# Splitting the last token tile's product and its evacuation into two column halves

## The chip, the cores and the metric

The kernel runs on one core of one Trainium2 chip. The metric is the device time of one execution in microseconds (us). I call the measured device time the clock. The profile shows one execution, whose span is some 1.7 us shorter than its device time. TensorE is PE in the profile, its weight loads PEld, VectorE is DVE, ScalarE ACT, GpSimd POOL, and SPq the queue from which the stores are issued.

All runs of more than one execution quoted here are of state fast; single runs have no state and are read from their traces alone. The sets of rounds ran on different chips, so a kernel is compared only with the kernel before of the same rounds.

## The reference, cut to what matters

A transformer block with modulation: sliding-window attention, then an MLP that mixes over tokens. Only the end of the MLP matters here (condensed from two functions).

```python
u = jnp.einsum('bsd,sf->bdf', h, w1) + b1      # S=2048 tokens, D=512, F=1792
u = _gelu(u)
y = jnp.einsum('bdf,fs->bds', u, w2) + b2      # second product: contracts F
x = x + gb * y.transpose(0, 2, 1)              # gate and residual, then out
```

## The kernel before

The output has 16 token tiles of 128 tokens by 512 columns. For each, TensorE sums 14 matmuls (128 rows of F each, 512 columns) into one PSUM buffer (pu). VectorE then does two instructions: f1, out of PSUM, adds b2 and multiplies by the gate; f2 adds the residual x and writes bf16 into an output buffer. A store of 128 KB sends it. The buffers o1 and otile rotate over three slots each.

```python
box["g"] = ctx.enter_context(tc.tile_pool(name="gtmp", bufs=3))
...
def e_f1(e, tb=tb):
    box["o1", tb] = box["g"].tile([P, D], F32, name="o1")
    ve.scalar_tensor_tensor(
        out=box["o1", tb][:], in0=ftiles[100 + tb], scalar=b2FM[:, tb : tb + 1], in1=bc_gb[:],
        op0=ALU.add, op1=ALU.mult,
    )

def e_f2(e, tb=tb):
    box["ot", tb] = box["g"].tile([P, D], BF, name="otile")
    ve.tensor_tensor(out=box["ot", tb][:], in0=box["o1", tb][:], in1=xres[tb][:], op=ALU.add)

def e_f3(e, tb=tb):
    sp.dma_start(out=out_dram[tb * P : (tb + 1) * P, :], in_=box["ot", tb][:])
```

The order of all pieces of work is a fixed list of numbers in the kernel; each engine works through its own instructions in that order. Its last entries read as follows (1366 is the residual add of tile 13, 1376 that of tile 14, 1378 to 1384 the last tile's matmuls in pairs, 1385 and 1386 its f1 and f2, 1367, 1377 and 1387 the stores of tiles 13, 14 and 15):

```
... 1373 1365 1357 1374 1380 1375 1381 1382 1376 1383 1366 1384
1385 1367 1377 1386 1387
```

So VectorE does tile 13's f1 (1365), tile 14's f1 (1375), and only then the two adds, 14's first.

The softmax here doesn't subtract the row's maximum and nothing guards it: scores larger than these inputs give would overflow.

## Time and profile before

| | before |
|---|---|
| device time, median | 267.24 us (267.21 to 267.50, 3 runs) |
| span of the profiled run (its device time 266.56) | 264.84 us |
| TensorE busy / VectorE busy | 94% / 73% |
| end of TensorE's last matmul | 260.60 us |
| last store issued / landed | 262.14 / 263.82 us |
| landing to the end of the span | 1.02 us |

The busy share of TensorE suggests that the body is bound by matmuls. The change is about the last 4.24 us, from the end of TensorE's last matmul to the end of the span; I call this stretch **R**. It is the sum of the wait and work on VectorE up to the last store's issue (1.54), the store's landing (1.68) and the closing waits (1.02).

### The profile page before, as it was taken

The page shows a single profiled execution, that of the slowest core. Times are in us where ns is not written, and L with a number is a line of the kernel's source. Part 1 is how long each engine was busy: PE and PEld are TensorE (multiplying, and loading weights), DVE is VectorE, ACT ScalarE, POOL GpSimd, SP SyncE. Part 2 cuts the span into 40 slices and gives each one's busy share as a digit, 9 for nine tenths or more (in the row PEclk, how much of TensorE's full clock was granted, in tenths as well). Part 3 has the DMA queues.
Part 4 walks back from the last instruction along what each step waited for, and adds up shares of the span by engine and source line. Part 5 has one row for each costly group of instructions (what it writes and reads, how often), then busy time and mean ns, then how long its engine had stood idle before and what let it go on. Part 6 is the DMA issues. An engine that isn't in the chain of part 4 may idle for free.

```text
span 264.8 us, 10695 instructions
## 1 busy us (share of the span) xinstructions
PE 248.2 (94%) x4769; PEld 136.8 (52%) x4769; DVE 193.5 (73%) x435; ACT 185.4 (70%) x268; POOL 95.9 (36%) x182
## 2 busy tenths in 40 slices
PE   7898999999998988899999999999999999999993
PEld 2576667656556654455544454445444444444441
DVE  5778896777847359999948888999998730415875
ACT  3479999999999899999999999999416431000000
POOL 8755321495289945553893031440000000000000
PEclk9999999999999999999999999999999999999999
DMA  7995400000017000000014862020499800001122
GB/s 212 369 382 197 42 5 6 2 5 2 2 49 196 5 4 5 2 2 2 5 38 128 227 172 85 2 61 23 152 362 397 360 2 0 21 0 63 59 99 79
DMA packets 31599, 25.35 MB, mean 96 GB/s; under 512 B 6076, under 2 KB 29632, under 8 KB 31552
## 3 DMA queue, kind: packets, MB, share of 16 engines
q1 hardware_dynamic: 31544, 24.66, 29.5%
q8 instruction: 37, 0.61, 0.9%
q14 instruction: 10, 0.08, 0.1%
q10 hardware_dynamic: 8, 0.00, 0.0%
HBM read 22.55 MB, written 2.10 MB: 93 GB/s over the span
## 4 chain that ended last, share of the span: by engine, by line
PE 67%; ACT 19%; DVE 8%; issue 4%; POOL 0%; ACTq 0%; POOLq 0%
PE pu L194 32%; ACT et L194 15%; PE pxy L194 13%; PE psa L194 8%; PE pq L194 5%; PE pa L194 4%; PE pv L194 3%; ACT lz L194 3%; DVE st L194 2%; DVE VT L194 1%; PE pt L194 1%; DVE part L194 1%; DVE OT L194 1%; PE psb L194 1%; DVE h L194 1%
## 5 line engine op out<-in xcount | busy, mean ns | idle before, releaser
L194 ACT ACTIVATE et<-psa 128x1536 bf16<-128x1536 f32 x75 | 109.1, 1455 | 4.0 <-PE psa L194 2.1
L194 PE MATMUL pu<-hb,w1p 128*128 128x512 bf16 x224 | 53.1, 380 | 0.8 <-DVE part L194 0.8
L194 PE MATMUL pu<-guT,w 128*128 128x512 bf16 x224 | 49.0, 379 | 0.0
L194 ACT ACTIVATE et<-psb 128x512 bf16<-128x512 f32 x75 | 45.1, 601 | 0.0
L194 PE MATMUL pxy<-et,ones_bd 128*32 128x192 bf16 (+3 forms) x960 | 38.7, 233 | 0.9 <-issue 0.9
L194 PE MATMUL pxy<-et,VT 128*32 128x192 bf16 (+3 forms) x960 | 38.4, 234 | 0.9 <-DVE OT L194 0.5
L194 PEld LDWEIGHTS <-w 128*128 128x128 bf16 x224 | 21.9, 98 | 26.4
L194 PE MATMUL psa<-QT,KT 32*128 32x192 bf16 (+3 forms) x720 | 29.8, 230 | 5.6 <-ACT et L194 4.9
L194 PEld LDWEIGHTS <-w1p 128*128 128x128 bf16 x224 | 20.3, 98 | 25.5 <-issue 2.3
L194 POOL TENSOR_SCALAR KT<-kb,mask_par 128x512 bf16<-128x512 bf16 (+1 forms) x36 | 22.9, 645 | 25.9 <-DVE kb L194 22.2
L194 PE MATMUL pq<-h1T,wqkv 128*128 128x512 bf16 (+1 forms) x128 | 30.1, 355 | 0.3 <-ACT VT L194 0.3
L194 PEld LDWEIGHTS <-KT 32*128 32x128 bf16 x960 | 16.1, 92 | 26.2 <-issue 23.9
L194 PEld LDWEIGHTS <-VT 128*32 128x32 bf16 x960 | 23.6, 96 | 11.6 <-issue 10.1
L194 PE MATMUL psb<-QT,KT 32*128 32x192 bf16 (+3 forms) x240 | 29.3, 231 | 0.0
L194 DVE SCALAR_TENSOR_TENSOR o<-pu,b2FM,bc_all 128x512 f32<-128x512 f32 x16 | 11.6, 748 | 20.2 <-PE pu L194 20.0
L194 DVE TENSOR_TENSOR et<-et,maskt 128x512 bf16<-128x512 bf16 (+2 forms) x56 | 24.9, 480 | 0.6 <-ACT et L194 0.5
L194 PEld LDWEIGHTS <-ones_bd 128*32 128x32 bf16 x960 | 23.2, 97 | 1.2 <-issue 1.1
L194 DVE BATCH_NORM_STATS2 st<-x 128x6 f32<-128x512 bf16 x32 | 21.7, 680 | 1.3 <-DMA x<-in_A_x_dram 1.1
L194 DVE TENSOR_TENSOR OT<-pxy,lz 128x256 bf16<-128x256 f32 x32 | 13.4, 420 | 10.6 <-ACT lz L194 10.1
L194 PEld LDWEIGHTS <-wqkv 128*128 128x128 bf16 x192 | 14.0, 97 | 13.4 <-issue 4.8
L194 PE MATMUL pv<-wqkv,h1T 128*32 128x256 bf16 x512 | 17.9, 274 | 0.2 <-DVE VT L194 0.2
L194 PE MATMUL pa<-wod,OT 128*128 128x512 bf16 x64 | 17.3, 381 | 0.3 <-ACT part L194 0.3
(113 smaller groups left out, 358.2 us busy)
## 6 DMA issues: line engine op xcount, KB each, us to landing
w1p<-in_B_w_dram SPq DMA_DIRECT2D x14, 512.0 KB, 6.1
w<-in_B_w_dram SPq DMA_DIRECT2D x14, 512.0 KB, 8.4
wmod<-in_w_mod_dram SPq DMA_DIRECT2D x6, 512.0 KB, 5.5
x<-in_A_x_dram SPq DMA_DIRECT2D x16, 128.0 KB, 4.8
out_dram<-otile SPq DMA_DIRECT2D x16, 128.0 KB, 1.7
wqkv<-in_A_wqkv_dram SPq DMA_DIRECT2D x2, 384.0 KB, 5.4
wqkv<-in_A_wqkv_dram SPq DMA_DIRECT2D x1, 512.0 KB, 5.0
wod<-in_A_wo_dram SPq DMA_DIRECT2D x1, 512.0 KB, 8.4
```

The costliest lines, as they stand in the source:

```text
L194: ins = call(*args, **kwargs)
```

## The change

The intent: the last tile's product is done in two column halves, each in a PSUM buffer of its own, the first half complete before the second begins. The first half's f1, f2 and store should go beside the second half's matmuls, so that only half of the evacuation follows TensorE's end. Its core (cuts marked):

```diff
-1385 1367 1377 1386 1387
+1367 1377 1385 1386 1387
...
+    def last_mm(e, n):
...
+        for m in range(4 * n, 4 * n + 4):
+            h, fc = divmod(m, NF)
+            te.matmul(
+                ftiles["last", h], lhsT=w2t[fc][:, (NT - 1) * P : NT * P], rhs=guT[fc][:, half * h : half * (h + 1)],
+                start=fc == 0, stop=fc == NF - 1, skip_group_check=True,
+            )
+
+    def last_out(h):
+        tb = NT - 1
+        cols = slice(half * h, half * (h + 1))
+        o1 = box["g"].tile([P, half], F32, name="o1h", tag="o1")
+        ot = box["g"].tile([P, half], BF, name="oth", tag="otile")
+        ve.scalar_tensor_tensor(
+            out=o1[:], in0=ftiles["last", h], scalar=b2FM[:, tb : tb + 1], in1=bc_gb[:, cols], op0=ALU.add, op1=ALU.mult,
+        )
+        ve.tensor_tensor(out=ot[:], in0=o1[:], in1=xres[tb][:, cols], op=ALU.add)
+        sp.dma_start(out=out_dram[tb * P : (tb + 1) * P, cols], in_=ot[:])
```

Both halves take their buffers from the same three slots as the whole tiles (tags o1 and otile). Entry 1385 of the list now stands for the first half's f1, f2 and store, 1386 for the second half's; so the halves' stores come after those of tiles 13 and 14.

More of the change, by code (lines that the diff above doesn't have):

```diff
@@ L1201 @@
         release(tag, ms, ge_ops[fc])
+    half = D // 2
+    def last_mm(e, n):
+        if n == 0:
+            for h in range(2):
+                ftiles["last", h] = box["ps_t"].tile([P, half], F32, name="pu1", tag=f"t{h}")[:]
+        for m in range(4 * n, 4 * n + 4):
[14 more added lines that the diff above has]
+        sp.dma_start(out=out_dram[tb * P : (tb + 1) * P, cols], in_=ot[:])
     fin_ops = {}
     for tb in range(NT):
+        if tb == NT - 1:
+            ms = []
+            for n in range(NF // 2):
+                ms.append(op("m2m", {"PE": 0.427}, lambda e, n=n: last_mm(e, n),
+                             deps=list(gu_ops.values()) + list(w2_ops.values()) + [fin_ops[t][0] for t in (10, 11)] + ms[-1:], pos=end + 17.0 + 3.0 * tb, cls="D"))
+            pos = end + 20.0 + 3.0 * tb
+            war = [fin_ops[t][2] for t in (tb - 3, tb - 2, tb - 1)]
+            f1 = op("f1", {"DVE": 0.76}, lambda e: last_out(0), deps=[ms[3]] + war, pos=pos)
+            f2 = op("f2", {"DVE": 0.76}, lambda e: last_out(1), deps=[f1, ms[-1]], pos=pos)
+            f3 = op("f3", {"SP": 0.64}, lambda e: None, deps=[f2], pos=pos, nbytes=64 * 1024)
+            fin_ops[tb] = (f1, f2, f3)
+            continue
         tag, ms = product("m2m", 100 + tb, [[(lambda fc=fc, tb=tb: w2t[fc][:, tb * P : (tb + 1) * P], lambda fc=fc: guT[fc][:]) for fc in (lo, lo + 1)]
```

## The prediction

> **What bounds the kernel now.** I first read the page's totals and its 40 slices (6.62 us each), to see which engine carries the last stage, then the chain of work that ended last, then the end of the timeline.
>
> ```profile
> PE 248.2 (94%) x4769; PEld 136.8 (52%) x4769; DVE 193.5 (73%) x435; ACT 185.4 (70%) x268; POOL 95.9 (36%) x182
> ...
> PE   7898999999998988899999999999999999999993
> ...
> DVE  5778896777847359999948888999998730415875
> ```
>
> The reader is to see two things. TensorE (PE) is busy nearly everywhere, so the body of the kernel is bound by it, and the change leaves its number of multiply-adds alone. In the last two slices VectorE (DVE) is at 7 and 5 tenths: at the very end it is not an idle engine waiting for the last product. The change can only act in the last microseconds, so the chain there is what counts:
>
> ```profile
> 5 pieces in order of time: start us, us, what
> 256.93 3.68 PE pu L194 x17
> 260.61 0.02 issue
> 260.63 0.76 DVE o L194
> 261.40 0.02 issue
> 261.42 0.69 DVE otile L194
> ```
>
> After TensorE's last matmul ends (260.61) come one scalar-tensor-tensor out of PSUM (o, bias and gate), one tensor-tensor (otile, the residual), then the store. This view ends at the last counted instruction; the store and the closing waits fill the rest of the 264.84 us. It suggests that TensorE's end releases everything, and that halving the two DVE instructions after it would save half of them. The timeline of VectorE over the same stretch shows why that is not so:
>
> ```profile
> 258.48 0.75 DVE L194 SCALAR_TENSOR_TENSOR o<-pu,b2FM,bc_all 128x512 f32<-128x512 f32 x1 [0.32 <-PE pu L194]
> 259.26 1.30 DVE L194 TENSOR_TENSOR otile<-o,x 128x512 bf16<-128x512 f32 x2
> 260.63 0.75 DVE L194 SCALAR_TENSOR_TENSOR o<-pu,b2FM,bc_all 128x512 f32<-128x512 f32 x1
> 261.42 0.69 DVE L194 TENSOR_TENSOR otile<-o,x 128x512 bf16<-128x512 f32 x1
> ```
>
> VectorE starts on token tile 14 at 258.48, then does the residual adds of tiles 14 and 13 until 260.56, and only then tile 15. Its work on the older tiles ends 0.05 us before TensorE's last matmul does: two chains end side by side. VectorE's backlog is as long as the product.
>
> The stores matter too. The timeline of the transfer queue over 260.5 to 260.9, and over 262.0 to the end:
>
> ```profile
> 260.58 0.33 SPq L194 DMA_DIRECT2D out_dram<-otile  x1
> ...
> 262.14 0.33 SPq L194 DMA_DIRECT2D out_dram<-otile  x1
> ```
>
> and the page's list of transfers (last column: us from issue to landing):
>
> ```profile
> out_dram<-otile SPq DMA_DIRECT2D x16, 128.0 KB, 1.7
> ```
>
> The first is the store of tile 13, whose landing the trace's records put at 262.30; one of tile 14 follows at 260.97 (lands 262.76); the last is that of tile 15, from 262.14 to its landing at 263.82. The span ends 1.02 us later.
>
> [...] the trace has 686 on average for otile. [...] the trace has a tensor-tensor of 256 columns:
>
> ```profile
> L194 DVE TENSOR_TENSOR OT<-pxy,lz 128x256 bf16<-128x256 f32 x32 | 13.4, 420 | 10.6 <-ACT lz L194 10.1
> ```
>
> [...] The trace has 216 between the starts of pu matmuls, and for four pq matmuls with 128x128 weights and 256 columns 0.60 us from first start to last end: (0.60 - 0.27)/3 = 0.11 between starts. So the doubled weight loads do not set the pace:
>
> ```profile
> 13.13 0.60 PE L194 MATMUL pq<-h1p,wqkv 128*128 128x256 bf16 x4
> ```
>
> [...] at the 160 GB/s or more that earlier slices show, 128 KB would move in under 0.8 us. I therefore expect a half-size store to land only slightly sooner. [...] Here VectorE is saturated for just these 2 us.
>
> **The change part by part.**
>
> TensorE: 14 matmuls of 512 columns become 28 of 256. 28 x 0.1085 = 3.04 against 14 x 0.216 = 3.02 us, so +0.02. The instruction listing shows 8 of the 28 before tile 14's last matmul, as 4 of the 14 were; so tile 14's release of VectorE stays within 0.01, and all ends near 260.63. The first half is complete 14 x 0.1085 = 1.5 us before that, about 259.1.
>
> VectorE: a scalar-tensor-tensor of 748 ns and a tensor-tensor of 686 become two of each with 256 columns. [...] 0.48 and 0.42. That is 1.80 for 1.43 us, +0.37.
>
> Buffers: the two halves take a slot each of the three otile slots, where the whole tile took one. The listing of waits shows that the first half's add waits for the store of tile 12 (landed 259.19, free), and the second half's add for the next store in order, tile 13's. That wait is new. Tile 13's store can't be issued before its add ends at 260.57, and this is unchanged.
>
> Now the times. The first half need not wait for the product, so it starts as soon as VectorE has issued tile 13's add: two adds in a row start 1.30 - 0.69 = 0.61 apart, so 259.87 + 0.61 = 260.48. Its add follows after 0.48 + 0.04 (a dependent pair starts 261.42 - 260.63 = 0.79 apart for a 0.75 first instruction): 261.00. The second half's first instruction starts 0.61 - 0.27 = 0.34 later, 261.34, long after its product is ready (260.63). Its add could go at 261.86. But tile 13's store lands at 262.30, and from a landing to the add that waits for it the trace has 0.09 (243.53 to 243.62). So it starts at 262.39, ends at 262.82 and its store is issued at 262.84: 0.70 later than the last store of before. I give the half-size store 1.62 instead of 1.68 to land. The sum is +0.70 - 0.06 = **+0.64 us**, and the clock for the whole program moves by the same.
>
> **The rivals.** (1) The intent works: the end follows the product, with 0.48 + 0.04 + 0.42 after it in place of 0.76 + 0.02 + 0.70. That would give -0.54, 266.7 us. Against it is the VectorE backlog: at 260.63 VectorE would be in the first half, which it started at 260.48 at the earliest. (2) VectorE alone is the bound and the buffer wait is harmless (another slot, or a store that lands sooner): the add goes at 261.86 and ends at 262.29, 0.17 later than the 262.12 of before; less 0.06 for the store, +0.1, 267.35 us. For it: the listing names only a transfer's lane, and I inferred the tile from the order of issue. (3) The 256-column matmuls are held up by their weight loads (98 ns busy each) and TensorE ends later: 28 x 10 ns would be 0.28, but 0.7 us of it are hidden behind VectorE, and only the 8 in front of tile 14's end push the rest, 0.08. (4) Two half stores (rows of 512 B in place of 1024 B) land no sooner or collide with the full stores of tiles 13 and 14: up to +0.1 to +0.3 more.
>
> **Range and chances.** 267.24 + 0.64 = 267.88; I say 267.85. The runs of before spread over 0.3 us, rival 2 lies at 267.35 and rival 4 at some 268.2, so 267.3 to 268.4 should hold 8 in 10. 2% is 5.3 us, more than everything from tile 14's first DVE instruction to the last landing except noise: same 0.98, each side 0.01.
>
> **What would show it.** Right: TensorE's last matmul ends at about 260.6 as before; VectorE shows four instructions of 128x256 of 0.48 and 0.42 us, the first starting near 260.5 without waiting for TensorE; the last add stands after an idle gap of some 0.5 us put down to a transfer out of otile; the last store is issued near 262.8. Wrong: the last add follows its partner at once (rival 2), or the span ends below 264.5, which would mean that VectorE had room for the first half before tile 13's add.

The forecast's sum came to +0.70 - 0.06 = +0.64 us. For 0.48 and 0.42, and for the 0.27 that follows from them, the trace of before gives the same values: an add takes 0.686 us at 512 columns and 0.420 at 256 (another tile's), 0.266 less, and 0.748 - 0.266 = 0.482 is then the estimate for f1. The 0.1085 us between the starts of matmuls of 256 columns lies within the 0.108 to 0.110 that the same trace has within its groups of pq matmuls. That a half-size store lands only slightly sooner was not shown: all 16 output stores of before have 128 KB, and the 1.62, so the -0.06 of the sum, is the author's guess. So are the 10 ns per matmul of rival 3 and the +0.1 to +0.3 of rival 4. "Saturated" stands for VectorE's 2.05 busy us of the 2.09 from 258.47 to 260.56.

## The result, and the profile after

The changed kernel took 267.88 us median (267.47 to 268.48, 4 runs); the kernel before, with one more run in the same rounds, 267.37 (267.21 to 267.59, 4 runs). The ratio is 1.002, with a 95% interval of 0.9998 to 1.0042. A ratio is the mean time of one kernel's fast runs over that of the other's of the same rounds, so not quite the ratio of the medians quoted. Kernels are compared only within the same rounds. By the 2% rule this is "same". The clock alone barely tells it from zero, so the traces decide.

First the totals and slices of the page of the changed kernel:

```profile
PE 249.0 (94%) x4783; PEld 138.2 (52%) x4783; DVE 194.2 (73%) x437; ACT 185.4 (70%) x268; POOL 95.8 (36%) x182
...
PE   7898999999989988799999999999999999999992
...
DVE  5768896777847559999948788999998730425865
```

There are 14 more matmuls and weight loads and 2 more VectorE instructions; nothing else in the body has changed. In the last slice VectorE still has 5 tenths, TensorE 2.

The end of the timeline of the changed kernel (start, duration, engine, instruction, count, and in brackets idle time before it and its releaser):

```profile
256.76 4.29 PE L194 MATMUL pu<-guT,w 128*128 128x256 bf16 x30
...
258.90 0.75 DVE L194 SCALAR_TENSOR_TENSOR o<-pu,b2FM,bc_all 128x512 f32<-128x512 f32 x1 [0.33 <-PE pu L194]
259.69 1.29 DVE L194 TENSOR_TENSOR otile<-o,x 128x512 bf16<-128x512 f32 x2
260.90 0.48 DVE L194 SCALAR_TENSOR_TENSOR o1h<-pu,b2FM,bc_all 128x256 f32<-128x256 f32 x1
261.41 0.42 DVE L194 TENSOR_TENSOR oth<-o1h,x 128x256 bf16<-128x256 f32 x1
261.75 0.48 DVE L194 SCALAR_TENSOR_TENSOR o1h<-pu,b2FM,bc_all 128x256 f32<-128x256 f32 x1
261.91 1.69 SPq L194 DMA_DIRECT2D out_dram<-oth  x2
262.82 0.42 DVE L194 TENSOR_TENSOR oth<-o1h,x 128x256 bf16<-128x256 f32 x1 [0.58 <-DMA out_dram<-otile]
```

TensorE ends at 256.76 + 4.29 = 261.05 (a merged row's duration runs from its first start to its last end). The first half starts at 260.90 without any wait on TensorE: its product was complete at 259.52 by the trace's records, but VectorE was at the adds of tiles 14 and 13 until then. So only 0.15 us of the first half's work lies beside the product. The second half's first instruction starts 0.71 after TensorE's end. Then VectorE stands idle for 0.58 us before the very last add, and what ends that idle time is a store out of otile.

The chain that ended last names the same thing:

```profile
260.30 0.70 DVE otile L194
261.00 0.02 issue
261.01 1.71 DMA out_dram<-otile
...
262.82 0.42 DVE oth L194
```

Before, the chain's last link to TensorE was the last matmul. Now it leads past it: tile 13's add (260.30), tile 13's store (1.71 us from issue to landing), the last add. None of TensorE's matmuls after 258.88, where tile 14's product ends, is on it. The view of the output's transfers matches only 12 of the 17 stores to their landings, and the last one is not among them. By the trace's records it is issued at 263.27 and lands at 264.80, 1.53 us later; the first half's store, which went while tile 14's was under way, took 1.62. R is 265.76 - 261.05 = 4.71 us, against 4.24 before. In parts: 2.22 up to the last issue (before 1.54), 1.53 of landing (1.68), 0.96 of closing waits (1.02); +0.68 - 0.15 - 0.06 = +0.47. TensorE's own time comes on top (next paragraph).

In this execution TensorE ended 0.45 us later than in the profiled execution of before. Nearly all of that was there long before the change: the first matmul of the second product (pu<-guT) starts at 211.21 in place of 210.79. From there to TensorE's end it is 49.84 us in every trace with the split product and 49.80 in the two without it (before, older_adds), so the change costs TensorE 0.04 us; to the end of the span it is 54.55 in place of 54.05, **+0.50 us** in all. Over all traces TensorE's end lies anywhere from 260.2 to 262.8 us, by turns for kernels that differ only in the tail, and this spread arises before the second product; why, I leave open. R, in contrast, repeats to 0.01 us where a kernel was traced more than once, so the experiments are read by it. Of the kernel before there is one trace.

### The profile page after: what moved, and what is told of

Same layout as the page of the kernel before. It is cut to its first block, busy times and chain, and to the rows that moved or that the text cites. A ratio compares the mean times of both kernels' runs of the same rounds, so it can differ in the third digit from the quotient of the medians.

```text
span 265.8 us, 10728 instructions
## 1 busy us (share of the span) xinstructions
PE 249.0 (94%) x4783; PEld 138.2 (52%) x4783; DVE 194.2 (73%) x437; ACT 185.4 (70%) x268; POOL 95.8 (36%) x182
## 4 chain that ended last, share of the span: by engine, by line
PE 66%; ACT 19%; DVE 8%; issue 4%; DMA 1%; POOL 0%; ACTq 0%; DVEq 0%; POOLq 0%
PE pu L194 31%; ACT et L194 15%; PE pxy L194 13%; PE psa L194 8%; PE pq L194 5%; PE pa L194 4%; PE pv L194 3%; ACT lz L194 3%; DVE st L194 2%; DVE VT L194 1%; PE pt L194 1%; DVE part L194 1%; DVE OT L194 1%; DMA out_dram<-otile 1%; PE psb L194 1%
## 5 line engine op out<-in xcount | busy, mean ns | idle before, releaser
L194 PE MATMUL pu<-guT,w 128*128 128x512 bf16 (+1 forms) x238 | 49.0, 366 | 0.0
L194 PEld LDWEIGHTS <-w 128*128 128x128 bf16 x238 | 23.3, 98 | 25.3
L194 DVE SCALAR_TENSOR_TENSOR o<-pu,b2FM,bc_all 128x512 f32<-128x512 f32 x15 | 10.9, 747 | 20.3 <-PE pu L194 20.2
```

The lines of the kernel that those rows point to most:

```text
L194: ins = call(*args, **kwargs)
```

## The experiments

My theory has two parts: (a) a backlog of VectorE, which hides the first half's early product, and (b) a wait for an output slot, which adds a store's landing to the path. Rivals: the split itself costs the time (more instructions, two stores, more weight loads), or the slot wait is the only obstacle.

The results in one table, all in us from the trace records. "Last add" and "last issue" count from the end of TensorE's last matmul.

| kernel | last add starts | last store issued | R |
|---|---|---|---|
| before | 0.83 | 1.54 | 4.24 |
| changed (three traces: 4.709, 4.709, 4.707) | 1.77 | 2.22 | 4.71 |
| own_slots | 1.22 | 1.67 | 4.16 |
| one_store | 1.22 | 1.67 | 4.36 |
| narrow_only | 0.82 | 1.54 | 4.23 |
| older_adds | 0.83 | 1.55 | 4.24 |
| early_add | 0.93 | 1.38 | 3.86 |
| own_and_adds | 0.65 | 1.11 | 3.58 |
| adds_shared | 0.64 | 1.10 | 3.58 |
| interleaved | 0.63 | 1.08 | 3.57 |
| own_o1 (two traces: 3.491, 3.493) | 0.56 | 1.01 | 3.49 |

All outputs were correct.

### after_again and after_third: the changed kernel once more

No edit.

> The changed kernel once more, with more rounds. Call T the stretch from the start of token tile 14's first VectorE instruction to the end of the span: in the first traces 258.48 to 264.84 = 6.36 us before, 258.91 to 265.76 = 6.85 us after. My theory (VectorE backlog, then a wait for the third output buffer) expects T = 6.85 again, an idle gap of 0.58 us before the last add, put down to a store out of otile, and about +0.5 us on the clock against before. The rival that the change costs nothing and the first difference was noise expects +0.0.

The clock: 268.39 us median (267.60 to 268.62, 6 runs), before 267.88 (267.09 to 268.66, 11 runs), ratio 1.0016 (0.9992 to 1.0040). T was 266.47 - 259.62 = 6.85, R 4.71.

> The changed kernel once more, on one chip with the best version, since the clock of single runs spreads by more than the effects. By the traces it ends 0.49 us later than before (R 4.71 for 4.24, TensorE 0.02 later): ratio 1.0018, R = 4.71 again.

267.40 us (267.12 to 267.80, 6 runs), before 267.20 (266.25 to 267.86, 11 runs), ratio 1.0017 (0.9998 to 1.0036). R was 4.71 a third time. Three sets of rounds give 1.0020, 1.0016 and 1.0017 where the traces say 1.0019 (+0.50 us). No single interval excludes 1. R does: 4.71 in three traces against 4.24 in the one of before, and 4.23 and 4.24 in narrow_only and older_adds below, which leave the last tile's evacuation whole.

### own_slots: the halves write output buffers of their own

```diff
-        ot = box["g"].tile([P, half], BF, name="oth", tag="otile")
+        ot = box["g"].tile([P, half], BF, name="oth", tag=f"oth{h}", bufs=1)
```

> The changed kernel, but each half writes an output buffer of its own, so that its add waits for no store. My theory: the last add follows its partner at once, 0.51 us after that one's start, T falls by the gap of 0.55 to 6.30 us, so 0.06 less than before and about 0.5 less than the changed kernel; no gain of 0.5 against before, because VectorE's backlog stays. The rival that the slot wait is harmless and the split itself costs the 0.5 us expects T = 6.85. The rival that the slot wait was the only obstacle and the intent then works expects T near 5.7.

```profile
261.53 0.48 DVE L194 SCALAR_TENSOR_TENSOR o1h<-pu,b2FM,bc_all 128x256 f32<-128x256 f32 x1
262.05 0.42 DVE L194 TENSOR_TENSOR oth<-o1h,x 128x256 bf16<-128x256 f32 x1
262.39 0.48 DVE L194 SCALAR_TENSOR_TENSOR o1h<-pu,b2FM,bc_all 128x256 f32<-128x256 f32 x1
262.90 0.42 DVE L194 TENSOR_TENSOR oth<-o1h,x 128x256 bf16<-128x256 f32 x1
```

In this timeline the last add follows its partner after 0.51 us, without an idle gap. T is 265.84 - 259.54 = 6.30, as the theory had it. The slot wait cost 0.55 us (R 4.71 to 4.16): part (b) is shown. But the intended gain of half a microsecond isn't there: R is only 0.09 below before. What is left is part (a). The clock gave 267.40 us median, ratio 0.9993 (0.9967 to 1.0019).

### one_store: one buffer and one store for both halves

```diff
-        ot = box["g"].tile([P, half], BF, name="oth", tag="otile")
+        if h == 0:
+            box["oth"] = box["g"].tile([P, D], BF, name="oth", tag="otile")
+        ot = box["oth"]
...
-        ve.tensor_tensor(out=ot[:], in0=o1[:], in1=xres[tb][:, cols], op=ALU.add)
-        sp.dma_start(out=out_dram[tb * P : (tb + 1) * P, cols], in_=ot[:])
+        ve.tensor_tensor(out=ot[:, cols], in0=o1[:], in1=xres[tb][:, cols], op=ALU.add)
+        if h == 1:
+            sp.dma_start(out=out_dram[tb * P : (tb + 1) * P, :], in_=ot[:])
```

> The changed kernel, but both halves write one output buffer and one store of 128 KB sends them, so no wait for a third buffer and no half-size store. Call R the stretch from the end of TensorE's last matmul to the end of the span: before 4.24, after 4.71, own_slots 4.16, own_and_adds 3.58 us. My theory: the last add at 1.22 us after TensorE's end as in own_slots, its store issued 0.13 later than before's, R = 4.37: the split of VectorE's work costs 0.13 where the backlog hides its gain, and the half-size store is worth 0.2. The rival that two stores instead of one are what costs expects R at or below before's 4.24.

```profile
262.88 0.42 DVE L194 TENSOR_TENSOR oth<-o1h,x 128x256 bf16<-128x256 f32 x1
263.33 0.33 SPq L194 DMA_DIRECT2D out_dram<-oth  x1
```

TensorE ended at 261.67 here, so the last add starts 1.22 later, as in own_slots, and the store goes at 1.67. R is 4.36 (one look). So VectorE's split alone costs 0.12 us against before where the backlog hides its use, and the second, half-size store gives 0.20 back (4.36 to 4.16): 0.14 by landing sooner (1.53 for 1.67) and 0.06 in the closing waits. There the store queue waits for the transfers' semaphores in a fixed order, some 0.06 us apart; by the records, four of these waits end after the last landing in before and one_store, three in the changed kernel and own_slots, where the last store signals on the next semaphore. So this 0.06 comes from one store more, not from its size. That two stores cost time is refuted.

### narrow_only: only TensorE's part

The last tile goes by 28 matmuls of 256 columns into the two halves of its one PSUM buffer (the record calls it a bank); evacuation and store stay whole.

```diff
+                if key == 100 + NT - 1:
+                    half = D // 2
+                    for m in range(4 * n, 4 * n + 4):
+                        h, fc = divmod(m, NF)
+                        te.matmul(
+                            ftiles[key][:, half * h : half * (h + 1)], lhsT=w2t[fc][:, (NT - 1) * P : NT * P],
+                            rhs=guT[fc][:, half * h : half * (h + 1)], start=fc == 0, stop=fc == NF - 1, skip_group_check=True,
+                        )
+                    return
```

> The kernel before with only TensorE's part of the change: the last tile's product by 28 matmuls of 256 columns into the two halves of its one bank, evacuated and stored whole. My theory: 28 starts 0.109 apart, so TensorE's end moves by 0.02 us, and R = 4.24 as before. The rival that the doubled weight loads hold up the matmuls expects starts over 0.115 us apart and TensorE's end later by 0.2 or more against tile 14's first VectorE instruction (2.12 us before).

The starts of the last 20 matmuls lie 0.109 us apart. Tile 14's first VectorE instruction stands 2.145 before TensorE's end, against 2.119 before, and R is 4.23 (one look). By this TensorE's part costs 0.03 us, and 0.04 counted from the second product's first matmul (49.84 against 49.80); the rival's 0.2 or more is refuted.

### older_adds and own_and_adds: VectorE's backlog taken away

Both give the residual adds of tiles 13 and 14 to GpSimd, which is idle there (for 82.9 us before the first of them, below), each right after its tile's first instruction; the second does so on top of own_slots.

```diff
-... 1373 1365 1357 1374 1380 1375 1381 1382 1376 1383 1366 1384
+... 1373 1365 1366 1357 1374 1380 1375 1381 1382 1376 1383 1384
...
-            ve.tensor_tensor(out=box["ot", tb][:], in0=box["o1", tb][:], in1=xres[tb][:], op=ALU.add)
+            (po if tb in (13, 14) else ve).tensor_tensor(out=box["ot", tb][:], in0=box["o1", tb][:], in1=xres[tb][:], op=ALU.add)
```

> The kernel before (no split), with the residual adds of token tiles 13 and 14 on the idle GpSimd in place of VectorE. My theory: alone it is worth nothing, T = 6.36 as before, since the last tile's first instruction waits for TensorE's last matmul anyway; VectorE merely becomes idle for some 1.3 us before it. The rival that the backlog of VectorE alone bounds the end expects T shorter by up to 0.1 us or more.

> The changed kernel with both obstacles gone: own output buffers for the halves, and the adds of tiles 13 and 14 on GpSimd. My theory: the first half is worked off before TensorE ends, the second half's first instruction waits for TensorE's last matmul, then 0.48 + 0.42 us and the half-size store: T = 5.6 us, 0.7 less than before. If the sum of the parts were additive (own_slots -0.06, older_adds 0.0), it would be T = 6.3: the difference is what only the two together give.

older_adds: R 4.24, as before; VectorE then idles 1.41 us before the last tile's first instruction. The clock's ratio was 0.9993 (0.9968 to 1.0017). So for the unsplit kernel the backlog costs nothing.

own_and_adds: R 3.58, which is 0.66 below before, where the parts taken one at a time give 0.09 (own_slots) and 0.00. The clock: 267.12 us (267.00 to 267.50, 6 runs), ratio 0.9975 (0.9956 to 0.9995). The backlog is what kept the split from working: part (a) is shown. T was 265.41 - 259.69 = 5.72 where 5.6 was expected. I put the missing 0.1 down to one line of this timeline, the first half's add; interleaved, below, shows that it is the smaller part:

```profile
259.50 2.27 POOL L194 TENSOR_TENSOR otile<-o,x 128x512 bf16<-128x512 f32 x2 [82.94 <-DVE o L194]
259.69 0.75 DVE L194 SCALAR_TENSOR_TENSOR o<-pu,b2FM,bc_all 128x512 f32<-128x512 f32 x1 [0.33 <-PE pu L194]
260.36 0.47 DVE L194 SCALAR_TENSOR_TENSOR o1h<-pu,b2FM,bc_all 128x256 f32<-128x256 f32 x1
260.87 1.19 DVE L194 TENSOR_TENSOR oth<-o1h,x 128x256 bf16<-128x256 f32 x1
261.98 0.47 DVE L194 SCALAR_TENSOR_TENSOR o1h<-pu,b2FM,bc_all 128x256 f32<-128x256 f32 x1
```

GpSimd works from 259.50 to 261.77. The first half's add, which takes 0.42 elsewhere, takes 1.19 and ends at 262.06, after GpSimd. The two first instructions beside GpSimd, which read PSUM, keep their 0.75 and 0.47. Only VectorE lost time: GpSimd's adds took 1.16 us each here, and 1.16 in interleaved with no VectorE add beside them. The expectations below call such an add one of two SBUF inputs: that is what it has and the first instructions lack. By what mechanism GpSimd's work slows it, the traces do not show.

### adds_shared: the backlog taken away, the slots left shared

The edit of older_adds on the changed kernel, so own_and_adds without the own buffers.

> own_and_adds without the buffers of their own: the changed kernel with only the adds of tiles 13 and 14 moved to GpSimd. R is the stretch from the end of TensorE's last matmul to the end of the span (own_and_adds 3.58, own_slots 4.16). If the slot wait came only from the backlog that delayed tile 13's store: that store is now issued 1.1 us before TensorE's end, lands 0.6 after it, and the last add, ready at 0.65, waits 0.0 to 0.1 us: R = 3.6. If the third slot is a cost of its own, R is nearer 4.1. And if two adds with two SBUF inputs each, on VectorE and GpSimd, hold each other up, the first half's add again takes some 1.19 us in place of 0.42.

```profile
259.26 1.19 DVE L194 TENSOR_TENSOR oth<-o1h,x 128x256 bf16<-128x256 f32 x1
260.37 0.47 DVE L194 SCALAR_TENSOR_TENSOR o1h<-pu,b2FM,bc_all 128x256 f32<-128x256 f32 x1
260.88 0.43 DVE L194 TENSOR_TENSOR oth<-o1h,x 128x256 bf16<-128x256 f32 x1
```

R 3.58 (one look), the same as with own buffers, and no gap before the last add. The slot wait is thus not a cost of its own: three slots are enough once tile 13's store is issued 1.15 us before TensorE's end instead of 0.04 before it. The backlog caused both losses. The 1.19 repeats.

### early_add: one number moved, VectorE alone

```diff
-... 1373 1365 1357 1374 1380 1375 1381 1382 1376 1383 1366 1384
+... 1373 1365 1366 1357 1374 1380 1375 1381 1382 1376 1383 1384
```

> The changed kernel with one number of the order moved: VectorE does tile 13's residual add right after tile 13's first instruction, in the 0.33 us in which it idled for tile 14's product, instead of after tile 14's. No GpSimd, no further buffer. My theory (a backlog of VectorE): its backlog shrinks by about 0.28 us, tile 13's store goes 1.7 us sooner and its landing no longer holds the last add; R = 3.88, 0.36 below before. A rival that only the slot wait counted expects R as in own_slots, 4.16.

```profile
257.60 0.75 DVE L194 SCALAR_TENSOR_TENSOR o<-pu,b2FM,bc_all 128x512 f32<-128x512 f32 x1
258.38 0.69 DVE L194 TENSOR_TENSOR otile<-o,x 128x512 bf16<-128x512 f32 x1
258.99 0.74 DVE L194 SCALAR_TENSOR_TENSOR o<-pu,b2FM,bc_all 128x512 f32<-128x512 f32 x1
259.77 0.69 DVE L194 TENSOR_TENSOR otile<-o,x 128x512 bf16<-128x512 f32 x1
260.38 0.48 DVE L194 SCALAR_TENSOR_TENSOR o1h<-pu,b2FM,bc_all 128x256 f32<-128x256 f32 x1
```

Tile 13's add fills the idle time before tile 14's product. TensorE ended at 260.82, so the first half starts 0.44 before it in place of 0.15. R is 3.86, 0.38 below before and 0.85 below the changed kernel, by an order alone. The clock: 266.66 us (265.93 to 267.38, 6 runs), before 267.18 (266.11 to 270.03, 11 runs), ratio 0.9979 (0.9937 to 1.0022), too wide to tell.

### interleaved and own_o1: a version that beats both

The changed kernel with own output buffers, tile 13's add on GpSimd, and VectorE's order: tile 14's first instruction, the first half's first, tile 14's add, the first half's add, then the second half. No add on VectorE then lies beside GpSimd's, and only the second half is still a pair of dependent instructions back to back.

```diff
-... 1373 1365 1357 1374 1380 1375 1381 1382 1376 1383 1366 1384
-1367 1377 1385 1386 1387
+... 1373 1365 1366 1357 1374 1380 1375 1381 1382 1383 1384
+1385 1376 1367 1377 1386 1387
...
-            f1 = op("f1", {"DVE": 0.76}, lambda e: last_out(0), deps=[ms[3]] + war, pos=pos)
-            f2 = op("f2", {"DVE": 0.76}, lambda e: last_out(1), deps=[f1, ms[-1]], pos=pos)
+            f1 = op("f1", {"DVE": 0.76}, lambda e: last_o1(0), deps=[ms[3]], pos=pos)
+            f2 = op("f2", {"DVE": 0.76}, lambda e: (last_out(0), last_o1(1), last_out(1)), deps=[f1, ms[-1]] + war, pos=pos)
```

(last_o1 is the first instruction of last_out, last_out the rest; tile 13's add goes to GpSimd as above.)

> The changed kernel with own buffers, tile 13's add on GpSimd (over before the halves' adds), and VectorE's order: tile 14's first, first half's first, tile 14's add, first half's add, then the second half. In own_and_adds the first half's add took 1.19 us in place of 0.42 while GpSimd was at tile 14's add, and held the second half by 0.11. My theory: here no VectorE add of two SBUF inputs lies beside a GpSimd add, so it takes 0.42 again, the second half starts 0.04 after TensorE's end, R = 3.48, 0.76 below before. The rival that the long add came from something else (the store, the buffer) expects it to stay at 1.19 and R at 3.58.

```profile
258.83 1.16 POOL L194 TENSOR_TENSOR otile<-o,x 128x512 bf16<-128x512 f32 x1 [82.94 <-DVE o L194]
260.67 0.42 DVE L194 TENSOR_TENSOR oth<-o1h,x 128x256 bf16<-128x256 f32 x1
261.27 0.48 DVE L194 SCALAR_TENSOR_TENSOR o1h<-pu,b2FM,bc_all 128x256 f32<-128x256 f32 x1 [0.18 <-PE pu L194]
```

R was 3.57, and the clock 266.46 us (266.42 to 266.89, 6 runs), ratio 0.9972 (0.9936 to 1.0009). The first half's add took 0.42 again, with the same buffers and a tile's store under way as in own_and_adds, so the rival for the long add is refuted. But the second half started 0.107 after TensorE's end, not 0.04. Its first instruction waited for two engines there: for TensorE, and for GpSimd's read of tile 13's o1, whose slot it takes. By the trace's records a semaphore instruction of its own waits for TensorE (until 0.042 after its end), and the instruction that then checks GpSimd, idle for 1.2 us, starts at 0.107. In own_and_adds, too, there were both waits, and the start was at 0.146; without the long add R fell by only 0.01 from there. own_o1 gives it a slot of its own (and lets the first half use the shared output slots again; with own slots for everything the pool needed 18 KB per partition where 17.2 were left, and did not build):

```diff
-        o1 = box["o1h", h] = box["g"].tile([P, half], F32, name="o1h", tag="o1")
+        o1 = box["o1h", h] = box["g"].tile([P, half], F32, name="o1h", **(dict(tag="o1h1", bufs=1) if h else dict(tag="o1")))
...
-        ot = box["g"].tile([P, half], BF, name="oth", tag=f"oth{h}", bufs=1)
+        ot = box["g"].tile([P, half], BF, name="oth", **(dict(tag="oth1", bufs=1) if h else dict(tag="otile")))
```

> The interleaved kernel, but the second half's first instruction writes a buffer of its own, so it waits for TensorE alone and no longer for GpSimd's add of tile 13 too (done 1.2 us earlier). In interleaved it started 0.107 after TensorE's end, in the kernel before 0.039. If checking a second semaphore costs this 0.07 although it is long satisfied, it starts at 0.04 here and R = 3.50 in place of 3.57, 0.74 below before. If not, R stays at 3.57.

The chain of own_o1 that ended last:

```profile
258.88 3.92 PE pu L194 x28
262.81 0.03 issue
262.83 0.49 DVE o1h L194
263.32 0.02 issue
263.35 0.43 DVE oth L194
```

This is what the change intended: TensorE's end, then half an evacuation, then a half-size store. The second half starts 0.039 after TensorE's end, R is 3.49: the second wait cost 0.07 us, the larger part of what was missing in own_and_adds. The clock: 266.29 us (265.87 to 268.02, 6 runs), before 267.04 (266.11 to 270.03, 12 runs), ratio 0.9962 (0.9921 to 1.0003). Again beside after_third:

> own_o1 once more, in the same rounds. By the traces R = 3.49 in place of 4.24 before: -0.75 us, with TensorE's 0.02 a ratio of 0.9973, and 1.2 us less than the changed kernel. If the clock shows no difference in this direction, R isn't what sets the time.

266.39 us (265.80 to 266.78, 6 runs), before 267.20, ratio 0.9978 (0.9957 to 0.9999), R 3.49. Against the changed kernel of the same rounds (267.40) it is 1.0 us faster by the medians, 1.21 by R. By the 2% rule every run is "same": the effects are under 0.5% of the clock.

## Why the prediction was right

It was right: 267.85 was predicted and 267.88 measured, "same" as forecast. That closeness is partly luck: the sum was 0.14 us too large, and the median of before was 0.13 higher in the result's rounds. The range rested on a spread of 0.3 us in three runs, where later rounds show the kernel before from 266.1 to 270.0. The steps are the better test, and the traces bear them out one by one, save for the half-size store's landing and the closing waits.

- **TensorE.** Its part was given as +0.02 us and was 0.03 to 0.04 (0.1085 us between starts was assumed, between the 0.108 and 0.110 of the pq matmuls of before; 0.109 was measured); the first half's product was complete early, and it didn't help.
- **VectorE's durations** of 0.48 and 0.42 us for 256 columns came out as 0.477 and 0.425.
- **The backlog.** The first half was to start 0.15 before TensorE's end (260.48 against 260.63) and started 0.15 before it. early_add and own_and_adds show that it was the backlog that held it.
- **The new wait.** The last add was to wait for tile 13's store; it did so for 0.58 us and started 0.09 after the landing (262.73 to 262.82), the distance read from the trace of before. I had inferred the tile from the order of issue; the chain names the store, and its issue at 261.01 follows the end of the second of the two adds, which the order makes tile 13's. own_slots takes the wait away and gets 0.55 back.
- **The last issue** was put 2.21 after TensorE's end (262.84 - 260.63) and came at 2.22.
- **The half-size store** is the term that was mis-sized: 1.62 us was guessed, 1.53 measured. The closing waits, taken as unchanged, fell by 0.06. So the traces say +0.50 where the sum said +0.64. (The prediction's estimate from the slices' 160 GB/s is 0.82 us for 128 KB, not under 0.8; no term was worked out from it.)
- **The rivals.** Rival 1 (the intent works) fails by the backlog. Rival 2 (no slot wait) is what own_slots makes of it: it said +0.1 and R fell by 0.09, the difference being the store and closing terms again. Rival 3 falls by narrow_only, rival 4 by one_store.

One thing the prediction did not see: both losses are one. I treated the backlog and the slot wait as two terms; adds_shared shows that with the backlog gone the shared slots cost nothing.

## What to carry to other kernels

Before halving the last tile so that its evacuation overlaps its product, look at whether the engine that evacuates is free at that moment: here the tail was two chains that ended together, and shortening one gave nothing (the backlog's removal alone, older_adds, gave 0.00 us, the split without its slot wait, own_slots, 0.09, both together 0.66). Splitting a tile also takes more buffer slots per unit of time, so ask which store the new piece waits for and when that store can be issued (here the last add stood 0.58 us idle for tile 13's store, issued 0.04 before TensorE's end). Where executions spread by more than the effect, measure the stretch of the trace that the change touches; it repeated to 0.01 us while the clock moved by 1 us and more.
